# Attention, an MLP and a routed expert layer in one kernel: gating in a queue of its own, the last batch's scores in single halves, and row copies ahead of gating at unit ends

## The chip, the cores and the metric

The kernel runs on one core of one Trainium2 chip. The metric is device time in microseconds (us) for one execution. Before the change the median of three runs is 875.8 us (875.69 to 875.85). TensorE (PE in the profile) does matrix products, VectorE (DVE) and ScalarE (ACT) the elementwise work, GpSimd (POOL) small operations and indirect DMAs, SyncE (SP) issues most DMAs. Products are accumulated in PSUM, which has eight banks here: six that the program calls acc0 to acc4 and px, and two called ph.

## The reference

What is computed, cut to its core (batch 4, 8 heads, sequence 576, head size 64, 32 memory slots; 2304 tokens of 512; MLP width 2048; 8 experts of width 1024):

```python
a = softmax(phi, over the sequence)
k_m, v_m = einsum(a, k), einsum(a, v)             # 32 memory rows per head
x = softmax(q @ k_m.T / 8) @ v_m                  # attention onto the 32 rows
x = elu(x @ w_in) @ w_out                         # dense MLP, all 2304 rows
noisy = x @ w_gate + log1p(exp(x @ w_noise)) * noise
w = softmax(top2(noisy))                          # two experts for each token
out[t] = sum of w[t, e] * (relu(x[t] @ w1[e]) @ w2[e])
```

## The kernel before

The work is a list of iterations `flat`, numbered i. Iterations 0 to 63 belong to four MLP units, one for each batch (16 iterations each; the batches' rows lie in blocks of 4, 5, 4 and 5 tiles of 128 rows). Iterations 64 to 95 belong to four "early" expert units (256 rows of experts 0 to 3, 8 iterations each), 96 to 159 to the remaining rows of these experts and to experts 4 to 7. In iteration i TensorE does layer 1 of i (`layer1`, L976, in two halves of the columns for the MLP) and layer 2 of iteration i - 2 (`layer2`, L1026 to L1028, three products for each row tile; high and low parts of the operands stand for one full-precision product). VectorE closes layer 1 with the ELU (`elu_b`, L990 and L991, twice each) and writes low parts (L1009 of the hidden rows, L574 of the weights). A ph bank is free for layer 1 of i + 1 only when the ELU of i has read it.

Everything else is side work fitted into these iterations:

- `attention(b)` of the next batch: phi turned (L175), memory rows, then for b of 2 and 3 the transposed scores, in four quarters (h, g): `scores_t` (matmuls L314), its shift by the maximum (L322 to L324 on VectorE), an exponential on ScalarE, `normalize_t` (L335 to L338, on VectorE for b = 3), `turn_t` (L342) and `lower_t` (L347). `fold` (L488) multiplies v_m into four chunks of w_in every fourth iteration; `halve` then makes a high (L137, ScalarE) and a low part (L138, VectorE).
- `gating(blk)`: the block's x rows are read back (`reload`, L813), each tile is transposed (L650) and multiplied with the gate weights (`logits`, L640 and the copy L642); then come the top two experts (L683 to L790) and list entries (L799, one DMA for each tile and choice).
- `fetch` (list of a unit L863, row gathers L880) and `spread` (four TensorE transposes for each gathered tile, L895) prepare the first early unit and the first unit behind the early ones; `route` (gathers L920, L925, L931 and later transposes by VectorE) prepares the rest at fixed half-iterations held in `plan`.

These are Python generators in two queues, `heads` and `tails`. `tick(slot)` is called at three places of an iteration ("" ahead of layer 1's operations, "mid" behind its last matmul, "late" behind the ELU and the weights' low parts) and lets the first generator whose next step wants that slot take it, at most a step or two a slot. `later` holds a step's PSUM reads back to the end of the VectorE work of layer 1 (`settle`). POOL's paced DMAs (list entries, gathers of `fetch`) wait in `spaced`; `beat()` releases one of them by a tiny ScalarE operation (L616) and a POOL copy of it (L617). `drain(gen)`, called at the first iteration of a unit, first issues everything in `spaced`, then runs the generator that the unit needs to its end. In single-bank stretches (`single()`: batches with five acc tiles in use) side work has only px, and a fold's second half uses a ph bank. At the end of a unit its acc tiles are copied out (`put_rows`, L1034 and L1036 for the MLP, L1045 and L1047 for experts), behind what the last "late" slot issued.

## Time and profile before

| what | value |
|---|---|
| median of three runs | 875.8 us |
| profiled execution, its own time | 877.42 us |
| its span from first to last instruction | 875.7 us |
| TensorE busy | 843.8 us, 96% |
| VectorE busy | 567.3 us, 65% |
| ScalarE busy | 438.4 us, 50% |
| GpSimd busy | 202.6 us, 23% |
| granted TensorE clock, mean | 0.991 |

The durations below are those of one execution. Rows of a time view give the start in us from the beginning of the span, the duration in us, engine, source line, operation, output <- inputs by the program's names, tile shapes, and in brackets the idle time of that engine just before it with what ended it. A merged row (x2, x4) has one start and the time until its last one ended. Operations overlap in their pipelines, so the distance of two starts is the better price of one. A granted clock of 1.00 is TensorE's upper level of 2.4 GHz; a stretch with a mean below that ran partly at 1.2 GHz.

### The profile page before, as it was taken

How to read it: one execution, taken by the hardware profiler on the slowest of the kernel's cores; microseconds unless marked ns; L12 is line 12 of the kernel's file. 1: busy time of each engine (PE TensorE's matmuls, PEld its weight loads, DVE VectorE, ACT ScalarE, POOL GpSimd, SP SyncE). 2: the span in 40 equal slices, each digit the busy share in tenths (PEclk: the TensorE clock that was granted, in tenths of full speed). 3: DMA queues.
4: the chain of work that ended last, by engine and by line, in shares of the span. 5: the costliest groups of instructions: out<-in, count | busy, mean ns of one | idle time of the engine just before them, and what ended most of it. 6: DMA issues, size and time to landing. Idle time of an engine off the chain costs nothing. (4 is left out here: it accounts for less than half of the span.)

```text
span 875.7 us, 15408 instructions
## 1 busy us (share of the span) xinstructions
PE 843.8 (96%) x5688; PEld 698.4 (80%) x5691; DVE 567.3 (65%) x1200; ACT 438.4 (50%) x1007; POOL 202.6 (23%) x319
## 2 busy tenths in 40 slices
PE   8999999999998999979989999999999999999995
PEld 5566567777876778868778998888899999999994
DVE  5878887689768887766787765655657444454321
ACT  4767666555664555545646654544444333342311
POOL 1000100001323147124327421322412050120303
PEclk9999999999999999999999999999999999999998
DMA  9996678963852346453789987878996675452404
GB/s 349 345 385 224 220 272 285 329 222 141 295 172 86 97 148 142 110 180 121 206 229 216 286 247 240 235 236 244 287 247 186 181 166 170 142 122 97 59 1 60
DMA packets 100575, 174.65 MB, mean 199 GB/s; under 512 B 14610, under 2 KB 52370, under 8 KB 99474
## 3 DMA queue, kind: packets, MB, share of 16 engines
q1 hardware_dynamic: 90514, 152.93, 54.7%
q0 software_dynamic: 9984, 20.72, 12.0%
q8 instruction: 45, 0.74, 0.3%
q14 instruction: 32, 0.26, 0.1%
HBM read 132.01 MB, written 41.61 MB: 198 GB/s over the span
## 5 line engine op out<-in xcount | busy, mean ns | idle before, releaser
L1026 PE MATMUL acc<-bh,gl 128*128 128x512 f32 (+1 forms) x552 | 220.1, 399 | 1.5 <-DVE rows L1047 1.4
L1027 PE MATMUL acc<-bl,gh 128*128 128x512 f32 (+1 forms) x552 | 216.3, 392 | 0.0
L1028 PE MATMUL acc<-bh,gh 128*128 128x512 f32 (+1 forms) x552 | 216.0, 391 | 0.0
L1005 DVE SCALAR_TENSOR_TENSOR gl<-ph,gh 128x312 fp32r<-128x312 f32 (+2 forms) x128 | 61.6, 482 | 195.0 <-ACT gh L1004 194.9
L568 ACT ACTIVATE bh<-raw 128x512 fp32r<-128x512 f32 x144 | 90.0, 625 | 71.0 <-PE acc L1028 71.0
L1026 PEld LDWEIGHTS acc<-bh,gl 128*128 128x128 f32 (+1 forms) x552 | 103.0, 187 | 27.4 <-issue 7.5
L1028 PEld LDWEIGHTS acc<-bh,gh 128*128 128x128 f32 (+1 forms) x552 | 102.9, 186 | 23.6
L1004 ACT ACTIVATE gh<-ph 128x312 fp32r<-128x312 f32 (+2 forms) x128 | 55.0, 430 | 124.5 <-PE ph L976 124.5
L1027 PEld LDWEIGHTS acc<-bl,gh 128*128 128x128 f32 (+1 forms) x552 | 103.1, 187 | 17.3
L1049 POOL DMA_INDIRECT out<-rows,ids x40 | 65.0, 1624 | 203.6 <-DVE rows L1047 168.3
L574 DVE TENSOR_TENSOR bl<-raw,bh 128x512 fp32r<-128x512 f32 x144 | 99.0, 688 | 6.1 <-ACT bh L568 6.1
L976 PE MATMUL ph<-xl,ah 128*128 128x312 f32 (+2 forms) x512 | 94.4, 306 | 0.0
L976 PE MATMUL ph<-xh,al 128*128 128x312 f32 (+2 forms) x512 | 93.8, 305 | 0.0
L976 PE MATMUL ph<-xh,ah 128*128 128x312 f32 (+2 forms) x512 | 93.7, 305 | 0.0
L976 PEld LDWEIGHTS ph<-xl,ah 128*128 128x128 f32 x512 | 83.0, 188 | 8.2
L976 PEld LDWEIGHTS ph<-xh,al 128*128 128x128 f32 x512 | 79.1, 188 | 0.0
L976 PEld LDWEIGHTS ph<-xh,ah 128*128 128x128 f32 x512 | 78.8, 188 | 0.0
L976 PE MATMUL ph<-tl,fh 128*128 128x288 f32 x256 | 61.7, 323 | 5.9 <-DVE elu L991 3.2
L574 DVE TENSOR_TENSOR al<-raw,ah 128x512 fp32r<-128x512 f32 x96 | 65.5, 682 | 0.0
L920 POOL DMA_INDIRECT xg<-x2d,ids x35 | 37.2, 1064 | 120.8 <-DMA ids<-lst 70.1
L990 DVE SCALAR_TENSOR_TENSOR elu<-elu 128x288 f32<-128x288 f32 x128 | 58.4, 456 | 9.2 <-ACT elu L982 9.1
L981 ACT ACTIVATE elu<-ph 128x288 f32<-128x288 f32 x128 | 52.3, 408 | 22.4 <-PE ph L976 21.1
(265 smaller groups left out, 1230.4 us busy)
## 6 DMA issues: line engine op xcount, KB each, us to landing
raw<-in_wmoe SPq DMA_DIRECT2D x48, 1024.0 KB, 6.1
raw<-in_wmlp SPq DMA_DIRECT2D x32, 512.0 KB, 5.4
raw<-wxa SPq DMA_DIRECT2D x12, 1024.0 KB, 6.0
raw<-wxb SPq DMA_DIRECT2D x12, 1024.0 KB, 5.6
xs<-xg SPq DMA_DIRECT2D x35, 256.0 KB, 6.4
xq<-xs SPq DMA_DIRECT2D x140, 64.0 KB, 4.9
kv<-in_kv SPq DMA_DIRECT2D x8, 1024.0 KB, 13.1
out<-zrow SPq DMA_DIRECT2D x13, 512.0 KB, 9.4
```

The costliest lines, as they stand in the source:

```text
L568: act.activation(ready[h, c][0], raws[h, c], AF.Copy)
L574: dve.tensor_tensor(lo, raws.pop((h, c)), hi.bitcast(F32), op=OP.subtract)
L920: pool.indirect_dma_start(out=xg, out_offset=None, in_=x2d[:rows], in_offset=bass.IndirectOffsetOnAxis(ap=n["ids"][:, t, 0:1], axis=0))
L976: pe.matmul(ph, w, x, start=k == 0, stop=k == len(terms) - 1)
L981: act.activation(t[:, 0, o], ph, AF.Exp)
L990: dve.scalar_tensor_tensor(m, t[:, 0, o], 1.0, m, op0=OP.add, op1=OP.mult)
L1004: act.activation(gh[:, o], ph, AF.Relu)
L1005: dve.scalar_tensor_tensor(gl[:, o], ph, 0.0, gh[:, o].bitcast(F32), op0=OP.max, op1=OP.subtract)
L1026: pe.matmul(acc, gl[:, o], wh, start=f == 0, stop=False)
L1027: pe.matmul(acc, gh[:, o], wl, start=False, stop=False)
L1028: pe.matmul(acc, gh[:, o], wh, start=False, stop=f == u["nf"] - 1)
L1049: d = pool.indirect_dma_start(out=out, out_offset=bass.IndirectOffsetOnAxis(ap=ids[:m, t, 0:1], axis=0), in_=r, in_offset=None, compute_op ...
```

## The change

Six edits; line numbers of the changed kernel differ from those above.

1. The per-tile part of gating (transpose, logits) becomes a generator `tiles` in a third queue `sides`; `gating` waits until its block's tiles are done. `sides` gets slots after the other two queues and can start while attention steps hold `heads`.
2. For b = 3 the scores are issued one quarter (h, g) an iteration instead of two, and their shift is put into `behind`, which is emptied behind the ELU.
3. `fetch` of the first early unit ends two steps later (`after` = 2), so that its `spread` starts later.
4. Where a unit ends, the "late" slot and its beat come behind `put_rows`.
5. `drain` issues beats only while the wanted generator is still queued.
6. A fold's halves change banks (the first half uses ph in single-bank stretches), and a fold inside layer 2 at a unit's first iterations comes after four tiles rather than three.

```diff
-    deferred, place = [], [""]
+    deferred, behind, place = [], [], [""]
...
             for g in gs:
-                later(lambda g=g: shift(g))
+                if place[0] == "mid" and not single():
+                    behind.append(lambda g=g: shift(g))
+                else:
+                    later(lambda g=g: shift(g))
...
-                    scores_t(h)
-                    yield "light"
-                    grow_t(h, 0)
-                    grow_t(h, 1)
-                    if h == 0:
-                        yield "mid"
+                    for g in range(2):
+                        scores_t(h, [g])
+                        yield "late"
+                        grow_t(h, g)
+                        if (h, g) != (1, 1):
+                            yield "mid"
...
-        bks = {g: bank("ph", 2) if single() and g else side_bank() for g in gs}
+        bks = {g: side_bank() if g or not single() else bank("ph", 2) for g in gs}
...
-    heads, tails, moe = [], [], {}
+    heads, tails, sides, moe = [], [], [], {}
...
-        for queue in (heads or tails, tails):
+        went = False
+        for queue in (heads or tails, tails, sides):
+            if queue is sides and slot == "mid" and not taken and not (went and single()):
+                kinds = {"mid"}
...
-                want = wants.get(id(gen)) or ("next" if gen.__name__ == "fetch" else "pe")
+                want = wants.get(id(gen)) or {"fetch": "next", "tiles": "late"}.get(gen.__name__, "pe")
...
     def drain(gen):
         place[0] = ""
-        while spaced:
-            beat()
         for queue in (heads, tails):
             while gen in queue:
+                while spaced:
+                    beat()
...
+    def tiles(blk, rows):
+        lg = att["lg", blk] = sm.tile([P, 5, 2 * NE], F32, tag="lg", name="lg", bufs=2)
+        for tt in range(BLOCKS[blk][1]):
             while tt >= len(rows):
                 yield "late"
             yield "late"
             x2T = rp.tile([P, 4, P], F32, tag="x2T", name="x2T", bufs=1)
             dve.transpose(x2T.rearrange("p g (a s) -> p a g s", s=32), rows[tt].rearrange("p a (g d) -> p a g d", d=32))
             yield "mid"
-            logits(tt, x2T, 1)
+            bk = side_bank()
+            logits(bk, x2T, 1)
+            later(lambda bk=bk, tt=tt: dve.tensor_copy(lg[:, tt, :], bk[:, :16]))
+        att["tiles", blk] = True
+
+    def gating(blk, rows):
...
+        while blk < 3 and ("tiles", blk) not in att:
+            yield "next"
...
-            if t == 3 and between:
+            if t == 3 + (f == 0) and between:
...
-                        (tails if k == 3 else heads).extend([fetch(n, [n]), n["need"]] if k == 3 else [n["need"]])
+                        (tails if k == 3 else heads).extend([fetch(n, [n], 2), n["need"]] if k == 3 else [n["need"]])
...
                 settle()
+                for f_ in behind:
+                    f_()
+                behind.clear()
...
-            tick("late")
-            if u["kind"] == "mlp":
-                beat()
+            ends = i >= LAG and pend[0][1] == pend[0][0]["nf"] - 1
+            if not ends:
+                tick("late")
+                if u["kind"] == "mlp":
+                    beat()
...
+                        sides.append(tiles(b, back))
...
+                if i < len(flat):
+                    tick("late")
```

What VectorE has in its row between the low parts of iteration 38 and the ELU of iteration 40, before (L322 to L324 are a quarter's shift, L990 and L991 the ELU, L1009 and L574 the low parts):

```order
L574 TENSOR_TENSOR bl<-raw,bh 128x512
L322 STREAM_TRANSPOSE sbt<-px 128x288
L323 TENSOR_REDUCE smx<-sbt 128x9
L324 TENSOR_TENSOR sbt<-sbt,smx 128x288
L322 STREAM_TRANSPOSE sbt<-acc_3138 128x288
L323 TENSOR_REDUCE smx<-sbt 128x9
L324 TENSOR_TENSOR sbt<-sbt,smx 128x288
L990 SCALAR_TENSOR_TENSOR elu<-elu 128x288
L991 SCALAR_TENSOR_TENSOR elu<-ph,elu 128x288
L990 SCALAR_TENSOR_TENSOR elu<-elu 128x288
L991 SCALAR_TENSOR_TENSOR elu<-ph,elu 128x288
L1009 TENSOR_TENSOR gl<-elu,gh 128x512
```

The same place in the changed kernel (L1006 and L1007 are the ELU, L652 a gating tile's transpose, L785 a gating reciprocal, L656 a logits copy):

```order
L1006 SCALAR_TENSOR_TENSOR elu<-elu 128x288
L1007 SCALAR_TENSOR_TENSOR elu<-ph,elu 128x288
L1006 SCALAR_TENSOR_TENSOR elu<-elu 128x288
L1007 SCALAR_TENSOR_TENSOR elu<-ph,elu 128x288
L322 STREAM_TRANSPOSE sbt<-px 128x288
L323 TENSOR_REDUCE smx<-sbt 128x9
L324 TENSOR_TENSOR sbt<-sbt,smx 128x288
L785 RECIPROCAL g_rec<-g_den 128x4
L652 STREAM_TRANSPOSE x2T<-xr 128x4x4x32
L1025 TENSOR_TENSOR gl<-elu,gh 128x512
L577 TENSOR_TENSOR bl<-raw,bh 128x512
L656 COPY lg<-acc_3262 128x16
```

Two shifts stood ahead of an ELU; now one stands behind it, with gating's transpose and copy in the same iteration.

ScalarE at the start of iteration 64, the first of the early units, before (L568 makes high parts of weights, L1004 the ReLU, L1034 copies rows out):

```order
L997 ACTIVATE gh<-elu 128x576
L1000 ACTIVATE gh<-rest 128x64
L616 ACTIVATE beat<-top 1x1 x8
L568 ACTIVATE ah<-raw 128x512
L568 ACTIVATE bh<-raw 128x512
L1004 ACTIVATE gh<-ph 128x256
L568 ACTIVATE ah<-raw 128x512
L568 ACTIVATE bh<-raw 128x512
L1004 ACTIVATE gh<-ph 128x256
L1034 ACTIVATE rows<-acc_4009 128x512
```

And in the changed kernel (L571, L1020, L1050 and L623 stand for L568, L1004, L1034 and L616):

```order
L1013 ACTIVATE gh<-elu 128x576
L1016 ACTIVATE gh<-rest 128x64
L571 ACTIVATE ah<-raw 128x512
L571 ACTIVATE bh<-raw 128x512
L1020 ACTIVATE gh<-ph 128x256
L571 ACTIVATE ah<-raw 128x512
L571 ACTIVATE bh<-raw 128x512
L1020 ACTIVATE gh<-ph 128x256
L623 ACTIVATE beat<-top 1x1
L1050 ACTIVATE rows<-acc_4017 128x512
```

The eight beats in a row are gone from there; single beats stand in the iterations behind.

GpSimd around the first early unit's two gathers (L880), before (L617 is a beat's copy, L799 a list entry, L690 a gating copy, L920 a routed unit's gather):

```order
L617 COPY tiny<-beat 1x1
L799 DMA lst<-g_rec,g_slot 19328x2
L690 COPY g_rec<-tokid 128x4 x2
L920 DMA xg<-x2d,ids 128x512
L617 COPY tiny<-beat 1x1
L880 DMA xg<-x2d,ids 128x512
L617 COPY tiny<-beat 1x1
L880 DMA xg<-x2d,ids 128x512
L920 DMA xg<-x2d,ids 128x512 x2
```

And in the changed kernel (L624, L815, L706, L896 and L936 in the place of these):

```order
L624 COPY tiny<-beat 1x1
L815 DMA lst<-g_rec,g_slot 19328x2
L624 COPY tiny<-beat 1x1
L896 DMA xg<-x2d,ids 128x512
L706 COPY g_rec<-tokid 128x4 x2
L624 COPY tiny<-beat 1x1
L896 DMA xg<-x2d,ids 128x512
L936 DMA xg<-x2d,ids 128x512 x4
```

Both gathers now stand ahead of the routed unit's and are released in iteration 58 rather than 59. The transposes that read them (`spread`) stood at the end of iteration 59 and inside 60 in TensorE's row; they now stand at the end of 60 and inside 61.

## Rows read from the trace of the kernel before

**Rows 1.** TensorE waits: who <- what it waited for: us, times, longest
```profile
PE px L895 <- DMA xg<-x2d,ids: 4.5, 1, 4.5
PE ph L976 <- DVE elu L991: 3.2, 3, 1.8
PE px L661 <- DVE rows L1036: 1.9, 1, 1.9
PE ph L976 <- DVE fl L138: 1.7, 3, 0.8
PE acc L1026 <- DVE rows L1047: 1.4, 1, 1.4
PE acc L640 <- DVE x2T L650: 1.0, 1, 1.0
```

**Rows 2.** stretches: length, busy us (count) by engine, clock, DMA, GB/s
```profile
234.00:314.00 80.00, 75.41 (x677) 58.50 (x677) 65.11 (x156) 44.38 (x129) 22.73 (x58) 0.98 0.44 130
375.00:393.00 18.00, 13.54 (x70) 11.89 (x69) 10.42 (x30) 6.64 (x18) 4.75 (x6) 0.91 0.70 220
```

**Rows 3.** TensorE in time: start us, us, line, operation, count; fold of iteration 50
```profile
326.63 1.04 PE L488 MATMUL px<-raw,vT 64*32 64x512 f32 x2
```

**Rows 4.** TensorE in time: scores by halves (batch 2), then by pairs (batch 3)
```profile
173.48 0.69 PE L314 MATMUL px<-q,kmF 64*32 64x288 f32 x8
174.10 0.50 PE L1026 MATMUL acc<-bh,gl 128*128 128x512 f32 x1
...
268.87 0.43 PE L314 MATMUL px<-q,kmF 64*32 64x288 f32 x1
...
269.52 0.50 PE L1026 MATMUL acc<-bh,gl 128*128 128x512 f32 x1
```

**Rows 5.** TensorE in time: first matmuls of iterations 36, 48 and 49
```profile
242.24 0.51 PE L976 MATMUL ph<-tl,fh 128*128 128x288 f32 x2
...
313.82 0.46 PE L976 MATMUL ph<-tl,fh 128*128 128x288 f32 x2
...
318.18 0.42 PE L976 MATMUL ph<-tl,fh 128*128 128x288 f32 x2
```

**Rows 6.** VectorE in time: start us, us; iterations 39 and 42
```profile
264.64 0.48 DVE L322 STREAM_TRANSPOSE sbt<-acc 128x288 f32<-128x288 f32 x1
...
266.02 0.45 DVE L990 SCALAR_TENSOR_TENSOR elu<-elu 128x288 f32<-128x288 f32 x1
...
284.40 0.45 DVE L990 SCALAR_TENSOR_TENSOR elu<-elu 128x288 f32<-128x288 f32 x1
...
286.11 0.45 DVE L335 TENSOR_REDUCE ssu<-sbt 128x9 f32<-128x288 f32 x1
...
287.43 0.70 DVE L650 STREAM_TRANSPOSE x2T<-xr 128x512 f32<-128x512 f32 x1
288.06 0.65 DVE L138 TENSOR_TENSOR fl<-px,fh 128x512 fp32r<-128x512 f32 x1
...
289.23 0.81 DVE L347 TENSOR_TENSOR tl<-back,th 128x288 fp32r<-128x288 f32 x2
...
289.95 0.68 DVE L1009 TENSOR_TENSOR gl<-elu,gh 128x512 fp32r<-128x512 f32 x1
...
291.24 0.45 DVE L990 SCALAR_TENSOR_TENSOR elu<-elu 128x288 f32<-128x288 f32 x1
```

**Rows 7.** GpSimd in time: the second gather of the first early unit
```profile
381.38 0.97 POOL L880 DMA_INDIRECT xg<-x2d,ids  x1 [0.48 <-issue]
```

**Rows 8.** ScalarE in time: beats at the start of iteration 64
```profile
408.43 0.46 ACT L616 ACTIVATE beat<-top 1x1 f32<-1x1 f32 x4
...
414.12 0.20 ACT L616 ACTIVATE beat<-top 1x1 f32<-1x1 f32 x1 [1.11 <-POOL tiny L617]
```

**Rows 9.** VectorE in time: a row copy of the first early unit
```profile
450.67 0.74 DVE L1047 TENSOR_SCALAR rows<-acc,ids 128x512 f32<-128x512 f32 x1
```

**Rows 10.** GpSimd in time: a routed unit's gather
```profile
518.95 0.99 POOL L920 DMA_INDIRECT xg<-x2d,ids  x1 [17.04 <-DMA xs<-xg]
```

More of the change, by code (lines that the diff above doesn't have):

```diff
@@ L601, in tick @@
                 stepped[id(gen)] = i
+                went = True
                 try:
@@ L629, in drain, with logits @@
                     wants.pop(id(queue.pop(0)), None)
-    def gating(blk, rows):
-        t0, nt = BLOCKS[blk]
-        lg = sm.tile([P, 5, 2 * NE], F32, tag="lg", name="lg")
-        def logits(tt, x2T, turned):
-            bk = side_bank()
-            for c in range(4):
-                for j in range(0, P, 32):
-                    pe.matmul(bk[j:j + 32, :16], x2T[:, c, j:j + 32], wgs[:, turned, c, :], start=c == 0, stop=c == 3,
-                              tile_position=(0, j))
-            later(lambda: dve.tensor_copy(lg[:, tt, :], bk[:, :16]))
-        x2T = None
-        for tt in range(nt if blk < 3 else 0):
+    def logits(bk, x2T, turned):
+        for c in range(4):
+            for j in range(0, P, 32):
+                pe.matmul(bk[j:j + 32, :16], x2T[:, c, j:j + 32], wgs[:, turned, c, :], start=c == 0, stop=c == 3,
+                          tile_position=(0, j))
+    def tiles(blk, rows):
+        lg = att["lg", blk] = sm.tile([P, 5, 2 * NE], F32, tag="lg", name="lg", bufs=2)
+        for tt in range(BLOCKS[blk][1]):
             while tt >= len(rows):
@@ L651, in gating @@
             yield "mid"
-            logits(tt, x2T, 1)
+            bk = side_bank()
[3 more added lines that the diff above has]
+    def gating(blk, rows):
+        t0, nt = BLOCKS[blk]
+        x2T = None
+        while blk < 3 and ("tiles", blk) not in att:
+            yield "next"
+        if blk == 3:
+            att["lg", blk] = sm.tile([P, 5, 2 * NE], F32, tag="lg", name="lg", bufs=2)
+        lg = att["lg", blk]
         for tt in range(nt + 1 if blk == 3 else 0):
             if tt:
-                logits(tt - 1, x2T, 0)
+                bk = side_bank()
+                logits(bk, x2T, 0)
+                later(lambda bk=bk, tt=tt: dve.tensor_copy(lg[:, tt - 1, :], bk[:, :16]))
                 if len(banks["tags"]) == 1:
```

## The prediction

> **What bounds the kernel now.** The table of engines comes first: TensorE is busy for 96% of the span, VectorE for 65%. So the time is TensorE's work, its few idle gaps, and what it loses at a low clock. The second view is TensorE's waits [rows 1]. The gaps that the change can touch are 4.5 us of `spread` for a gather, 3.2 us of layer 1 for the ELU (three times, the longest 1.8), 1.9 us of the last block's turn for a row copy, 1.7 us of layer 1 for the folded weights' low part (three times), 1.4 us of layer 2 for an expert's row copy, and 1.0 us of the logits for a transposed tile. The third view is the table of stretches [rows 2]: the mean clock is 0.98 over 234 to 314 and 0.91 over 375 to 393. At 1.2 GHz work takes twice as long as at 2.4, so a missing share of 0.02 in 80 us is 1.6 us lost, and 0.09 in 18 us is also 1.6. In each of the two lies one of the longest gaps (1.8 and 4.5 us); with a gap gone I count its clock loss as gone too. Then I read TensorE and VectorE in time inside those stretches.
>
> Waits and clock together are 13.7 + 3.2 = 16.9 us; that is the pool from which the change can draw, apart from TensorE work that it adds.
>
> **The change part by part.**
>
> *Folds (edit 6).* In single-bank stretches the folded half that layer 1 wants first was the second to be lowered; now it is the first. Two low parts take 1.17 us (288.06 to 289.23 in [rows 6]), so one of them 0.6. Of the three waits of 1.7 us in all [rows 1] two are longer than that: each falls by 0.6, the third (0.1 to 0.2) goes. In iteration 50 the fold also stands one tile later; its first matmuls take 1.04 us there [rows 3], while their partners wait for the ELU to free a ph bank. How much of it is waiting no other row here shows: bounds 0 and 1.0; I take 0.7. Sum: 0.6 + 0.6 + 0.15 + 0.7 = -2.0.
>
> *Scores and gating tiles (edits 1 and 2).* Iterations 36 to 47 take 313.82 - 242.24 = 71.6 us [rows 5], a bare one 318.18 - 313.82 = 4.4. In 39 and 40 two shifts of 1.38 us each (264.64 to 266.02) stand ahead of the ELU, and the next layer 1 waits for it. After the change only one shift an iteration is left, behind the ELU. VectorE then has in 39: ELU 1.7, shift 1.4, transpose 0.6, low parts 1.2 and small things, about 5.2; TensorE has 4.4 + 0.6 (scores) + 0.5 (logits) = 5.5 there. So the waits there go: -3.2 of the ELU waits, -1.0 at the logits, whose transpose is done an iteration ahead, and the clock loss of 1.6. Removed: 5.8.
>
> What is added is, first, TensorE work. A quarter issued alone takes 174.10 - 173.48 = 0.62 us, a pair 269.52 - 268.87 = 0.65 [rows 4]. Two pairs become four single quarters: 4 x 0.62 - 2 x 0.65 = +1.2. The Trainium skill ("TensorE: Matmul & The Clock Gate", section "Why this matters for your kernels", small-K matmuls) says that products with a short contraction which lie in separate row groups run at the same time, which speaks against splitting them. The trace agrees, 0.65 for a pair beside 0.62 for one; without that rule the split would cost nothing, and the sum would be 1.2 lower.
>
> Second, VectorE's work is not less, it is later. From [rows 6]: ELU 284.40 to 286.11 = 1.7; a normalization to 287.43 = 1.3; a transposed gating tile 0.6; two folded low parts 1.2; two lowers (289.23 to 289.95) 0.7, and two turns, which have the same shape, 0.7 too; the iteration's low parts and a logits copy to 291.24 = 1.3. By the order, iteration 42 has ELU, shift, folded parts, normalization, low parts: 1.7 + 1.4 + 1.2 + 1.3 + 1.2 = 6.8. 43 has ELU, normalization, turns, low parts: 4.9 and a small reciprocal; 44 the lowers instead of the turns, 4.9; 45 normalization and turns, 4.9; 46 lowers, two gating steps, folded parts, low parts, 5.6. In all 27.1 or a little more. TensorE has in 42 to 46 five bare iterations, 22.0, two folds of 1.1 and one quarter, 24.8. VectorE becomes the bound there, by at least 27.1 - 24.8 = 2.3 us. It also stands idle in 42 until the fold, which ends the iteration, has been read by ScalarE: no row gives the price of that at this place, so 0 and 2.2 bound it. New waits: 2.3 to 4.5; I take 3.0, since iteration 41 leaves VectorE a lead of under one us. Sum of the stretch: -5.8 + 1.2 + 3.0 = -1.6, with -4.6 (none) and -0.1 as ends. The reloads that feed gating's transposes are issued as before; the transposes come up to three iterations earlier. If one came before its data, the wait would be of the size of the 1.0 at the logits [rows 1]; I count nothing.
>
> *First early unit (edit 3).* The second gather is issued at 381.38 [rows 7] and its transposes wait 4.5 us. After the change the gathers are released an iteration earlier and read one later, two iterations or some 10 us more between them, so the wait goes whole, and with it the clock loss of 375 to 393: -4.5 - 1.6 = -6.1. Nothing else waits on them: the unit's first layer 1 is three iterations behind the last transpose.
>
> *Beats at 64 (edit 5).* Eight beats hold ScalarE from 408.43 to 414.32 [rows 8], each waiting for GpSimd's copy. ScalarE's ReLUs come late, VectorE's row copies behind them too, and the turn waits 1.9 us [rows 1]. With the flush gone ScalarE goes on at 408.5. Bounds: 0, if VectorE is late for another reason, and 1.9 and the end of the lateness. I take -1.9.
>
> *Row copies first (edit 4).* The copy at 450.67 takes 0.74 us [rows 9] behind six small gating operations, and layer 2 waits 1.4 for it. The copy itself stays, so the wait falls to 0.7 at best: -0.7. At the other unit ends no such wait is in [rows 1]; there late work, gating's POOL and ScalarE steps among it, only goes behind.
>
> Sum: -2.0 - 1.6 - 6.1 - 1.9 - 0.7 = -12.3. The profiled execution, 877.42 by its own time (span 875.7), would come to 865.1; the median of the runs lies 1.6 below the profiled execution, 875.8 - 12.3 = 863.5.
>
> **The rivals.**
>
> *R1, no new wait on VectorE.* If the shifts and normalizations of 42 to 47 fit (the engine starts 42 with a lead, and each ELU is needed only at the next layer 1's end of ph), the 3.0 goes: 860.5. For it: VectorE's share of the stretch is 65.1 of 80 us [rows 2]. Against: the sum of 27.1 beside 24.8.
>
> *R2, the clock falls again.* New waits in 43 to 47 that gather into one of 1.8 us or more cost 1.6 each, as the old ones did [rows 1, 2]: 865.1, and with two 866.7. The skill ("TensorE: Matmul & The Clock Gate", section "HAM oscillation — how this bites in real kernels") tells of kernels that pay such a fall again in every loop, behind waits for data. Here the traces show two falls; without that sentence the rival stands on [rows 2].
>
> *R3, edit 3 doesn't do what it says.* If the gathers, released by beats, wait for their list and slide along with the transposes, the 6.1 stays: 869.6. Against: GpSimd's order has both ahead of a routed gather that stood between them.
>
> *R4, slower: beats against GpSimd's waits.* The eight list entries flushed at 64 are now spread over 66 to 70, in the row of GpSimd with routed gathers. Such a gather has held GpSimd 17.0 us, until its data was stored [rows 10]. If one stands between two beats, the ring of four beats fills, ScalarE stops at the next beat, and its ReLUs with it; TensorE runs on to the end of its iteration on its two ph banks, half a bare iteration or 2.2 us in the mean [rows 5]. 17.0 - 2.2 = 14.8 us: 863.5 + 14.8 = 878.3. From a hold of 14.5 us on the kernel is slower than before (12.3 + 2.2). Against: that hold is at 519, where a unit of five tiles is routed; near 420 there is none among TensorE's waits.
>
> **How the numbers follow.** The forecast 0.54, R1 0.16, R2 0.13, R3 0.08, R4 0.07, others 0.02 (of it half slower). Forecast 863.5, by its own bounds 860 to 867 (the fold's 0.7, the beats' 1.9, VectorE's 2.3 to 4.5). R1 and R2 lie inside or near 859 to 867; R3 takes the upper end to 870; R1 with the higher gains of the folds and beats takes the lower one to 858. The range is 858 to 870. A measurement of this kernel tells 0.2%, 1.75 us, from no change. Faster by more than that: everything below 874, 0.54 + 0.16 + 0.13 + 0.08 less an allowance of 0.04 for two mishaps together, 0.87. Slower, above 877.6: half of R4 and others with what ends there, 0.08; the rest, 0.05, lies within.
>
> **What would show it.** In the profile after: no wait at `spread`, a clock of 1.00 over the last MLP iterations (edit 3); no eight beats at the start of 64 and no wait at the last block's first turn (edit 5); layer 1's waits for the folded low part at 0.3 or less (edit 6); one wait of about 0.7 where layer 2 follows the first early unit's row copies; in 36 to 47 some 70 us, with no layer 1 waiting for the ELU in 39 to 41 and small waits for it in 43 to 47. A mean clock above 0.995 says that no fall came back. What would prove me wrong: a wait for the ELU that is as long as before in 39 to 41, a wait at `spread`, or a TensorE gap behind 66 that ends with ScalarE.

## The result and the profile after

The changed kernel takes 866.5 us (median of four runs, 866.2 to 867.1) beside 875.75 for the kernel before: a ratio of 0.990, with a 95% interval of 0.988 to 0.992, or 9.2 us. Forecast were 863.5, inside a range of 858 to 870, and 12.3. The profiled execution of the changed kernel took 866.58 us with a span of 864.8; its mean clock is 0.998.

The engines' line of the page after:

```profile
PE 840.4 (97%) x5688; PEld 695.7 (80%) x5691; DVE 567.5 (66%) x1200; ACT 438.3 (51%) x1007; POOL 205.5 (24%) x319
```

TensorE's waits after, the view of [rows 1] (who <- what it waited for: us, times, longest). The program's lines are shifted by up to 16: L992 is layer 1, L1007 the ELU, L768 and L770 the count products of gating, L1042 layer 2, L1063 an expert's row copy.

```profile
PE ph L992 <- DVE elu L1007: 4.7, 4, 1.7
...
PE acc L768 <- DVE fl L138: 1.5, 1, 1.5
PE acc L770 <- DVE g_oh L759: 1.2, 1, 1.2
...
PE acc L1042 <- DVE rows L1063: 0.5, 1, 0.5
PE ph L992 <- DVE fl L138: 0.5, 1, 0.5
```

The 4.5 us at `spread` and the 1.9 at the last block's turn are gone, the folded low part is down from 1.7 to 0.5, the row copy from 1.4 to 0.5. But the waits for the ELU, 3.2 before, are 4.7, and 1.5 us are new, at gating's count products (L768; the 1.2 at L770 stood in the kernel before too, at its L754). The stretches that answer to [rows 2], same columns:

```profile
234.00:310.00 76.00, 71.58 (x666) 55.83 (x650) 62.20 (x153) 44.48 (x128) 26.14 (x59) 1.00 0.44 130
365.00:390.00 25.00, 25.00 (x151) 21.10 (x150) 20.07 (x58) 14.69 (x40) 6.74 (x10) 1.00 0.54 179
```

The clock is 1.00, the upper level, in both, where it was 0.98 and 0.91. TensorE in time (start, duration, in brackets the wait before), the start of iteration 36 and the waits of 36 to 47:

```profile
239.66 0.51 PE L992 MATMUL ph<-tl,fh 128*128 128x288 f32 x2
...
259.99 0.18 PE L768 MATMUL acc<-run,ones 128*128 128x40 bf16 x1 [1.47 <-DVE fl L138]
...
288.87 0.50 PE L992 MATMUL ph<-tl,fh 128*128 128x288 f32 x2 [1.25 <-DVE elu L1007]
...
294.62 0.53 PE L992 MATMUL ph<-tl,fh 128*128 128x288 f32 x2 [1.17 <-DVE elu L1007]
...
299.80 0.54 PE L992 MATMUL ph<-tl,fh 128*128 128x288 f32 x2 [0.53 <-DVE elu L1007]
...
311.74 0.50 PE L992 MATMUL ph<-tl,fh 128*128 128x288 f32 x2 [1.72 <-DVE elu L1007]
```

The first is the start of iteration 36, the last the start of 48: 311.74 - 239.66 = 72.1 us, beside 71.6 in [rows 5].

To see where the time went, I cut the runs' traces at TensorE's first layer 1 product of an iteration; in us:

| iterations | before | changed | difference | forecast |
|---|---|---|---|---|
| up to 15 | 124.7 | 123.7 | -1.0 | 0 |
| 16 to 35 | 117.5 | 116.0 | -1.5 | -1.2 |
| 36 to 47 | 71.6 | 72.1 | +0.5 | -1.6 |
| 48 to 55 | 44.2 | 42.7 | -1.4 | -0.8 |
| 56 to 62 | 44.7 | 38.4 | -6.4 | -6.1 |
| 63 to 74 | 50.2 | 48.0 | -2.2 | -2.6 |
| 75 to 95 | 60.65 | 61.2 | +0.6 | 0 |
| 96 to 127 | 129.2 | 128.9 | -0.3 | 0 |
| 128 to 158 | 209.1 | 210.5 | +1.4 | 0 |

The first line is scatter: up to 15 the programs have the same work, and over all profiles here that part ran from 122.5 to 125.8. Without it the sum is -9.3; the end of the program, behind the start of 159, is another 0.5 shorter. Against the forecast two things are missing: 2.1 us in 36 to 47, and 1.7 in the expert iterations, where I had expected nothing to change.

### The profile page after: what moved, and what is told of

Same layout as the page of the kernel before. It is cut to its first block, busy times and chain, and to the rows that moved or that the text cites. A ratio compares the mean times of both kernels' runs of the same rounds, so it can differ in the third digit from the quotient of the medians.

```text
span 864.8 us, 15414 instructions
## 1 busy us (share of the span) xinstructions
PE 840.4 (97%) x5688; PEld 695.7 (80%) x5691; DVE 567.5 (66%) x1200; ACT 438.3 (51%) x1007; POOL 205.5 (24%) x319
## 5 line engine op out<-in xcount | busy, mean ns | idle before, releaser
L1042 PE MATMUL acc<-bh,gl 128*128 128x512 f32 (+1 forms) x552 | 219.6, 398 | 0.6 <-DVE rows L1063 0.5
L571 ACT ACTIVATE bh<-raw 128x512 fp32r<-128x512 f32 x144 | 89.9, 624 | 72.5 <-PE acc L1044 72.4
L1042 PEld LDWEIGHTS acc<-bh,gl 128*128 128x128 f32 (+1 forms) x552 | 102.8, 186 | 26.2 <-issue 6.5
L1020 ACT ACTIVATE gh<-ph 128x312 fp32r<-128x312 f32 (+2 forms) x128 | 54.8, 428 | 126.1 <-PE ph L992 125.9
L992 PE MATMUL ph<-xl,ah 128*128 128x312 f32 (+2 forms) x512 | 95.2, 308 | 0.0
L992 PE MATMUL ph<-xh,al 128*128 128x312 f32 (+2 forms) x512 | 94.2, 306 | 0.0
L992 PE MATMUL ph<-xh,ah 128*128 128x312 f32 (+2 forms) x512 | 93.5, 305 | 0.0
L992 PEld LDWEIGHTS ph<-xl,ah 128*128 128x128 f32 x512 | 83.5, 189 | 8.9
L992 PEld LDWEIGHTS ph<-xh,al 128*128 128x128 f32 x512 | 79.4, 188 | 0.0
L992 PEld LDWEIGHTS ph<-xh,ah 128*128 128x128 f32 x512 | 78.9, 188 | 0.0
L992 PE MATMUL ph<-tl,fh 128*128 128x288 f32 x256 | 60.5, 317 | 6.3 <-DVE elu L1007 4.7
L1006 DVE SCALAR_TENSOR_TENSOR elu<-elu 128x288 f32<-128x288 f32 x128 | 58.5, 457 | 9.4 <-ACT elu L998 9.4
L936 POOL DMA_INDIRECT xg<-x2d,ids x35 | 37.3, 1066 | 112.7 <-DMA ids<-lst 70.4
L1013 ACT ACTIVATE gh<-elu 128x576 fp32r<-128x576 f32 (+1 forms) x50 | 33.0, 660 | 58.4 <-DVE elu L1007 58.4
```

Of the source, the lines that this page charges most:

```text
L571: act.activation(ready[h, c][0], raws[h, c], AF.Copy)
L936: pool.indirect_dma_start(out=xg, out_offset=None, in_=x2d[:rows], in_offset=bass.IndirectOffsetOnAxis(ap=n["ids"][:, t, 0:1], axis=0))
L992: pe.matmul(ph, w, x, start=k == 0, stop=k == len(terms) - 1)
L1006: dve.scalar_tensor_tensor(m, t[:, 0, o], 1.0, m, op0=OP.add, op1=OP.mult)
L1013: act.activation(gh[:, o], m, AF.Copy)
L1020: act.activation(gh[:, o], ph, AF.Relu)
```

## The experiments

All times are medians, beside the kernel before in the same group of runs. There are three groups: in the first (the four kernels down to the count products) the kernel before took 878.5 us, in the others 875.8 and 875.4, so times are compared within a group, or as ratios. Runs with profile have their stretches in the table behind the experiments.

**One edit alone, on the kernel before.** Edit 3:

```diff
-extend([fetch(n, [n]), n["need"]]
+extend([fetch(n, [n], 2), n["need"]]
```

> The kernel before with edit 3 alone: the first early unit's transposes stand one to two iterations later, its gathers where they were. Theory (the parts of the change add up): the 4.5 us wait and the clock fall behind it go, -6.1 us beside the kernel before, and iterations 59 to 62 have no wait. Rival (the wait goes only because the gathers also came earlier, by edit 1): a wait of 1 us or more is left, -3 to -5 us.

874.7 us beside 878.5, ratio 0.995 (0.993 to 0.996). The 3.8 us lie in the rival's range, but the wait that the rival leaves isn't there: nothing waits at `spread`, and 56 to 62 take 39.4 instead of 44.7, -5.4. So edit 3 does it without the earlier gathers. But 63 to 74 take 52.9 rather than 50.2. TensorE in time there:

```profile
415.64 0.66 PE L661 MATMUL px<-ident,rows 128*128 128x128 f32 x4 [2.52 <-DVE bl L574]
...
417.22 1.06 PE L976 MATMUL ph<-xh,ah 128*128 128x256 f32 x4
```

The turn of the last block waits 2.5 instead of 1.9, and four products of 256 columns behind it last 1.06 in all where four before them last 0.71: a fall to 1.2 GHz that the kernel before had not here. Whether the edit brings these 2.7 us is not shown: the kernels of this group are long there whatever the edit (below), and the kernel before has no profile in this group.

Edit 6:

```diff
-bks = {g: bank("ph", 2) if single() and g else side_bank() for g in gs}
+bks = {g: side_bank() if g or not single() else bank("ph", 2) for g in gs}
...
-if t == 3 and between
+if t == 3 + (f == 0) and between
```

> The kernel before with edit 6 alone: the first needed half of a fold uses the ph bank, and the fold of iteration 50 stands one tile later. Theory: the three waits for the folded low part fall by 1.3 us and the fold of 50 gains up to 1.2, -2.0 to -2.7 us. Rival (the fold's gain in the changed kernel came from VectorE's lighter load by edits 1 and 2): less than 1 us.

877.3 us beside 878.5, ratio 0.998 (0.997 to 1.000). 16 to 35 give 1.5, all of what the change gives there, 48 to 55 give 0.6 of the 1.4; the rest of it comes with edits 1 and 2, which take six small gating operations of VectorE out of 48 to 51. By the stretches, 2.1 together, the theory holds at its lower end; the time alone, 1.3 shorter with an interval of 0.4 to 2.5, does not tell it from the rival. The trace has one thing more, in a stretch that this edit does not touch:

```profile
142.37 0.53 PE L976 MATMUL ph<-tl,fh 128*128 128x288 f32 x2 [0.51 <-DVE fl L138]
...
419.15 0.66 PE L661 MATMUL px<-ident,rows 128*128 128x128 f32 x4 [1.49 <-issue]
```

The first row is the wait for the folded low part, 0.83 before. The second is a wait of 1.5 for nothing that the profile shows. Edits 3 and 6 alone take 2.7 and 3.5 us more in 63 to 74 than the kernel before elsewhere, the count step later (below) 3.4 more than the changed kernel elsewhere, and three of the four kernels of this group have waits of this kind (0.85 to 1.5). I come back to it in the last section.

Edits 1 and 2 (the other four undone in the changed kernel):

```diff
-extend([fetch(n, [n], 2), n["need"]]
+extend([fetch(n, [n]), n["need"]]
...
-        bks = {g: side_bank() if g or not single() else bank("ph", 2) for g in gs}
+        bks = {g: bank("ph", 2) if single() and g else side_bank() for g in gs}
...
-            if t == 3 + (f == 0) and between:
+            if t == 3 and between:
...
-            ends = i >= LAG and pend[0][1] == pend[0][0]["nf"] - 1
+            ends = False
...
-                if i < len(flat):
-                    tick("late")
```

and `drain` as before.

> The kernel before with edits 1 and 2 alone (gating tiles in their own queue, the last batch's scores by quarters). Theory: the waits for the ELU only move from iterations 39 to 41 to 43 to 47, and a new wait of 1.5 us stands at gating's count step behind the fold of iteration 38, so no gain: between -0.5 and +1 us. Rival (the prediction's sum, with the missing microseconds lost elsewhere): -1.6 us or more.

875.4 us beside 878.5, ratio 0.996 (0.995 to 0.997). The 3.1 us are the rival's number, but not for its reason: 36 to 47 take 72.5, +0.9, as the theory had it; what falls is 56 to 62, by 3.9, and iteration 65, from 7.3 to 5.25. TensorE at the first early unit's transposes, and GpSimd's two gathers for them:

```profile
370.52 0.63 PE L911 MATMUL px<-ident,xg 128*128 128x128 f32 x4 [1.32 <-DMA xg<-x2d,ids]
```

```profile
366.82 1.12 POOL L896 DMA_INDIRECT xg<-x2d,ids  x1 [1.22 <-issue]
...
369.32 0.98 POOL L896 DMA_INDIRECT xg<-x2d,ids  x1 [0.50 <-issue]
```

With gating's tiles in their own queue the entries of the list are done earlier, the gathers go out some twelve us earlier (the second at 369.3 rather than 381.4 [rows 7]), and the wait is 1.3 instead of 4.5, though the transposes come earlier too, in 57 and 58. It is edit 1 that does this: with edit 2 undone (below) the gathers are issued in 57 and 58 too, with edit 3 alone in 59 and 60. So edits 1 and 3 both act on this wait: -3.9 with edits 1 and 2, -5.4 with edit 3 alone, together -6.4. And the eight beats at 64 are gone with edits 1 and 2, though `drain` is as before.

**The count products.** The changed kernel with one step moved:

```diff
-        yield "next" if blk < 2 else "pe"
+        yield "next" if blk == 1 else "pe"
```

> The changed kernel with one step moved: the count products of the first block's gating want the slot that a fold closes, so they stand an iteration behind the fold of 38 and not right behind it. Theory: the 1.5 us wait for the folded low part at the count step goes and nothing takes its place: 865.0 us, 1.5 below the changed kernel. Rival (the wait is slack that layer 1 of 39 would have spent anyway, waiting for the same VectorE row): same time, and a wait of 1 us or more at layer 1 of iteration 39 or 40.

867.9 us beside 878.5, ratio 0.988 (0.986 to 0.989); the changed kernel's is 0.990 (0.988 to 0.992) in its own groups, so the times alone do not show a gain. Inside the stretch the theory holds: iteration 38 goes from 7.7 to 6.0, 39 from 5.6 to 5.8, 36 to 47 from 72.1 to 70.5. The two banks that side work has there, acc4 and px, both hold the fold; the count products are next in TensorE's row and need one of them, so they wait until ScalarE and VectorE have read it. What is left, and this group's wait for nothing:

```profile
286.95 0.50 PE L992 MATMUL ph<-tl,fh 128*128 128x288 f32 x2 [1.07 <-DVE elu L1007]
...
413.87 0.45 PE L642 MATMUL acc<-wgs,x2T 128*32 128x16 f32 x32 [0.85 <-issue]
```

**The changed kernel again, and its addresses.**

> The changed kernel itself, once more, so that the next kernels have it beside them on the same chip. Theory and rival alike: 0.987 to 0.992 of the kernel before.

866.6 us beside 875.8; ratio 0.990 (0.988 to 0.991).

```diff
+    sm.tile([P, 48], F32, tag="pad", name="pad")
```

> The changed kernel with an unused tile of 192 bytes a partition among the small tiles, so that the tiles behind them lie 512 bytes from where they lay in the kernel before, rather than 320. Nothing else differs. Theory: the second logits buffer of the change moved the expert operands, and their matmuls became slower by that (an iteration of 256 rows 2.82 to 2.85 us instead of 2.79, one of 624 rows 6.88 instead of 6.83, some 27 and 31 of them); with the pad they are back at 2.79 and 6.83, the kernel 2 to 2.4 us faster than the changed one. Rival (the expert iterations are slower for another reason, such as DMA traffic moved by the change): same iterations, same time.

864.7 us beside 866.6, ratio to before 0.987 (0.985 to 0.989). First products of early iterations and of two late ones, TensorE in time; before, after, and with the pad:

```profile
435.65 0.63 PE L976 MATMUL ph<-xl,ah 128*128 128x256 f32 x4
...
438.44 0.63 PE L976 MATMUL ph<-xl,ah 128*128 128x256 f32 x4
...
653.76 0.73 PE L976 MATMUL ph<-xl,ah 128*128 128x312 f32 x4
...
660.59 0.74 PE L976 MATMUL ph<-xl,ah 128*128 128x312 f32 x4
```

```profile
424.29 0.65 PE L992 MATMUL ph<-xl,ah 128*128 128x256 f32 x4
...
427.13 0.64 PE L992 MATMUL ph<-xl,ah 128*128 128x256 f32 x4
...
429.95 0.65 PE L992 MATMUL ph<-xl,ah 128*128 128x256 f32 x4
...
642.04 0.75 PE L992 MATMUL ph<-xl,ah 128*128 128x312 f32 x4
...
648.92 0.75 PE L992 MATMUL ph<-xl,ah 128*128 128x312 f32 x4
```

```profile
424.73 0.63 PE L994 MATMUL ph<-xl,ah 128*128 128x256 f32 x4
...
427.52 0.63 PE L994 MATMUL ph<-xl,ah 128*128 128x256 f32 x4
...
430.31 0.63 PE L994 MATMUL ph<-xl,ah 128*128 128x256 f32 x4
...
642.19 0.74 PE L994 MATMUL ph<-xl,ah 128*128 128x312 f32 x4
...
649.02 0.74 PE L994 MATMUL ph<-xl,ah 128*128 128x312 f32 x4
```

Distances of starts: 256 rows, 2.79 before, 2.84 and 2.82 after, 2.79 and 2.79 with the pad; 624 rows, 6.83, 6.88 and 6.83. 75 to 95 and 128 to 158 are back at 60.7 and 209.1. The theory holds: the second buffer of `lg` moved everything behind the small tiles by 320 bytes, and these iterations pay 0.7 to 1.8% for it. Not all expert operands lie behind the small tiles: by the addresses in the built programs the rows and the weights of layer 1 moved, the hidden rows and the weights of layer 2 did not. 192 bytes that nobody uses give 1.9 us by the medians, 1.7 by the stretches. The next run says more: its unused tile of 768 bytes makes the shift 1088, and 75 to 95 and 128 to 158 take 61.2 and 210.6 there, as in the changed kernel.

**VectorE as the bound of 43 to 47.** Three fills (`junk`, 192 columns) of 0.26 us, 0.78 together, behind the ELU of five iterations of the changed kernel:

```diff
                 behind.clear()
+                if i in (39, 40, 41, 44, 45):
+                    for _ in range(3):
+                        dve.memset(junk, 0.0)
```

> The changed kernel with three small extra VectorE fills (a few tenths of a us together) behind the ELU of iterations 39, 40, 41, 44 and 45. The computation is the reference's. Theory (VectorE bounds 43 to 47 and not 39 to 41): iterations 39 to 41 stay at 5.5 to 5.6 us, 44 and 45 grow by what the fills take. Rival (the waits in 43 to 47 come from ScalarE's or GpSimd's side of the chain): all five stay as they are.

868.75 us in one run, +2.2; 36 to 47 take 74.5, +2.5. The fills on VectorE in 41 and 44, then TensorE's waits at the starts of 44, 46 and 47:

```profile
277.37 0.87 DVE L1230 MEMSET junk<- 128x192 f32 x3
...
295.45 0.87 DVE L1230 MEMSET junk<- 128x192 f32 x3
```

```profile
288.92 0.50 PE L993 MATMUL ph<-tl,fh 128*128 128x288 f32 x2 [1.68 <-DVE elu L1008]
...
300.80 0.53 PE L993 MATMUL ph<-tl,fh 128*128 128x288 f32 x2 [1.46 <-DVE elu L1008]
...
307.11 0.54 PE L993 MATMUL ph<-tl,fh 128*128 128x288 f32 x2 [0.64 <-DVE elu L1008]
```

39 and 40 stay at 5.62 and 5.52; 41 grows by 0.2, and 43 by 0.4, with the wait at the start of 44 from 1.25 to 1.68. 45 and 46 grow by 0.95 and 0.7, together 1.65 for 1.6 of fills in 44 and 45: as the theory had it, one iteration later than it said. So VectorE is the bound from 43 on and has slack ahead of it. The slack is small: the fills of 39 and 40 cost nothing, and of the 0.78 in 41 about 0.65 comes out.

**Edit 2 undone in the changed kernel** (scores in pairs again, shifts ahead of the ELU):

```diff
-                if place[0] == "mid" and not single():
-                    behind.append(lambda g=g: shift(g))
-                else:
-                    later(lambda g=g: shift(g))
+                later(lambda g=g: shift(g))
...
-                    for g in range(2):
-                        scores_t(h, [g])
-                        yield "late"
+                    scores_t(h)
+                    yield "light"
```

> The changed kernel with edit 2 undone (the last batch's scores in pairs, their shifts ahead of the ELU), edit 1 kept. Theory (edit 2 only moves VectorE's excess from 39 to 41 into 43 to 47): waits of 1.2 us or more for the ELU at the starts of 40 and 41 with a clock below 1.00 behind them, none above 0.6 in 44 to 48, iterations 36 to 47 within 1.5 us of the changed kernel's 72.1, the time within 1.5 us of it. Rival (edit 2 is what removes the clock fall and costs nothing that stood before): 3 us or more slower than the changed kernel.

867.2 us beside 875.4, ratio 0.990 (0.989 to 0.991), as the changed kernel's. 36 to 47 take 72.4. The times are the theory's; the waits are not where it had them:

```profile
271.21 0.45 PE L639 MATMUL acc<-wgs,x2T 128*32 128x16 f32 x32 [1.50 <-DVE sbt L322]
...
291.98 0.65 PE L989 MATMUL ph<-tl,fh 128*128 128x288 f32 x2 [2.30 <-DVE elu L1004]
...
292.90 0.68 PE L989 MATMUL ph<-th,fh 128*128 128x288 f32 x2
```

```profile
234.00:310.00 76.00, 70.12 (x658) 55.59 (x658) 62.93 (x157) 43.74 (x127) 25.16 (x60) 0.98 0.42 120
```

TensorE waits 0.6 and 1.5 at the logits in 39 and 40, for the shift that still reads their bank, not for the ELU; and 2.3 in one piece at the start of 44, after which the clock falls to 1.2 GHz (a pair of products of 288 columns 0.68 rather than 0.43; mean clock 0.98 over the stretch, 1.00 with edit 2). So edit 2 turns waits of 0.6, 1.5 and 2.3 into four of at most 1.7, of about the same sum. It saves a clock fall and pays for it with TensorE work; the stretch is as long.

**Edit 5 undone in the changed kernel:**

```diff
         place[0] = ""
+        while spaced:
+            beat()
         for queue in (heads, tails):
             while gen in queue:
-                while spaced:
-                    beat()
```

> The changed kernel with edit 5 undone (all spaced DMAs issued at the start of 64). Theory: the few beats left there hold ScalarE again and iteration 65 goes from 5.24 back to about 7.3: +2 us. Rival (fewer beats are spaced at 64 since gating is later, so the flush is short): under 0.7 us.

867.4 us, ratio 0.991 (0.989 to 0.992). The rival holds, and further than it went: the built program has the same instructions in the same order on every engine as the changed kernel. At 64 nothing is spaced any more: with edits 1 and 2 the eight list entries come into the queue later, and go out one or two at a time in 65 to 70. It is therefore a third measurement of the changed kernel, and says that a median here is good to about 1 us.

**Combined versions.** The pad, the count step, the second block's gating delayed by two iterations, and the fold's lowering put behind the side step that follows:

```diff
-                place[0] = ""
+                place[0] = "mid"
                 fold(j // 4, j % 4, [0, 1])
             tick("", turn_ if i > 13 else i % 2 == 0)
+            settle()
...
-        for _ in range(3 if eng is pool else 0):
+        for _ in range(5 if eng is pool and blk else 3 if eng is pool else 0):
```

> The changed kernel with four edits: the pad; the first block's count step one slot later; the second block's gating steps two iterations later, out of 46; and a fold's lowering put behind the side step that follows it, so that a normalization fills VectorE's wait for the fold in 42. Theory: -2.2 (pad), -1.5 (count step), -1.2 (wait of 1.25 at iteration 44), -1.5 (wait of 1.72 at iteration 48): 860 us on the chip where the changed kernel takes 866.5, a ratio of 0.983 to the kernel before. Rival (the waits for the ELU only move on to the next iterations, since the steps of the chain are the same in number): pad and count step alone, ratio 0.986.

863.25 us, ratio 0.986 (0.984 to 0.988): the rival's number, but not for its reason. 36 to 47 fall to 68.7, -3.4 (iteration 43 from 5.8 to 4.4, 47 from 6.3 to 5.5, 38 from 7.7 to 6.0). Given back are 0.4 in 35, 0.35 in 36, 0.9 in 50 and 51, and 1.75 in 62 and 63, where one of the first early unit's gathered tiles is now transposed and count products wait (0.6 of it has only moved there, out of 60 and 61):

```profile
392.63 0.18 PE L772 MATMUL px<-g_oh,tri 128*128 128x32 bf16 x1 [0.94 <-DVE g_oh L761]
```

The next version confines the fold's delay to one fold and shortens `fetch` by one step; the one behind it keeps the delay of that fold, the pad and the count step alone:

```diff
-                place[0] = ""
+                place[0] = "mid" if i == 43 else ""
...
-fetch(n, [n], 2)
+fetch(n, [n], 1)
```

> The combined kernel with two of its edits cut to where they pay: the fold's lowering behind the side step at iteration 42 alone, and the first early unit's fetch one step shorter, so that its transposes stand at the ends of 60 and 61 as in the changed kernel. Theory: keeps the combined kernel's gains in 38, 43 and 47 (1.7, 1.4, 0.8) and the pad's 1.9, and loses none of the 0.75 in 35 and 36, 0.9 in 50 and 51, 1.4 in 60 to 63: 861 us where the changed kernel takes 866.5, ratio 0.983. Rival: its second gather is issued about 5 us ahead of its transposes, and lands later, a wait of 1 to 2 us at 61: 862 to 863.

> As the one before, without the two iterations' delay of the second block's gating steps, and with the fetch as in the changed kernel. Theory: the wait of about 1.7 at the start of 48 stays, no risk at 61: 861.8 us, ratio 0.984. Rival: as the waits of 43 to 47 hang together, the wait at 48 grows by what 44 gains (1.4): 863.

The two take 862.8 and 863.1 us beside 875.4, ratios 0.985 (0.984 to 0.986) and 0.985 (0.984 to 0.987). Both are faster than either kernel of the case; between themselves they cannot be told apart. The times are the two rivals' numbers, for other reasons. The first has 68.3 in 36 to 47 and 38.4 in 56 to 62 without a wait at `spread`, so its rival's cause falls; the second has 69.2 in 36 to 47. Its theory holds: the wait at the start of 48 is 1.74, no more than in the changed kernel. The waits for the ELU left in the first:

```profile
292.48 0.53 PE L994 MATMUL ph<-tl,fh 128*128 128x288 f32 x2 [1.11 <-DVE elu L1009]
...
297.67 0.53 PE L994 MATMUL ph<-tl,fh 128*128 128x288 f32 x2 [0.51 <-DVE elu L1009]
...
308.81 0.50 PE L994 MATMUL ph<-tl,fh 128*128 128x288 f32 x2 [0.95 <-DVE elu L1009]
```

The forecasts of 861 and 861.8 were too low by 1.8 and 1.3. In the first of the two, two stretches are not as forecast: 50 and 51 are still 0.9 longer than in the changed kernel, and 96 to 127 are 0.4 longer than with the pad alone, for a cause that stays open. The second has neither, and its wait at the start of 48 is 1.74 instead of 0.95. So delaying the second block's gating only moves VectorE's work for it: 0.8 won at 48 and 0.9 lost at 50 and 51. The stretches of the second are as forecast. The rest is the start: the profiled spans, 861.9 and 861.4, began with 124.4 and 124.7 us up to 15, and the changed kernel's with 123.5 and 123.7. That part scatters, as said.

| us in iterations | 16 to 35 | 36 to 47 | 48 to 55 | 56 to 62 | 63 to 74 | 75 to 95 | 96 to 127 | 128 to 158 |
|---|---|---|---|---|---|---|---|---|
| before | 117.5 | 71.6 | 44.2 | 44.7 | 50.2 | 60.65 | 129.2 | 209.1 |
| changed | 116.0 | 72.1 | 42.7 | 38.4 | 48.0 | 61.2 | 128.9 | 210.5 |
| edit 3 alone | 117.5 | 71.6 | 44.2 | 39.4 | 52.9 | 60.7 | 129.2 | 209.1 |
| edit 6 alone | 116.1 | 71.6 | 43.6 | 45.8 | 53.8 | 60.65 | 129.2 | 209.1 |
| edits 1 and 2 alone | 117.5 | 72.5 | 43.45 | 40.9 | 51.25 | 61.8 | 129.0 | 210.55 |
| changed, count step later | 116.1 | 70.5 | 42.7 | 38.4 | 51.4 | 61.3 | 129.0 | 210.6 |
| changed, pad | 116.1 | 72.0 | 42.75 | 38.4 | 47.9 | 60.7 | 129.2 | 209.1 |
| changed, edit 2 undone | 116.05 | 72.4 | 43.0 | 38.4 | 47.7 | 61.2 | 129.0 | 210.6 |
| combined, second version | 116.0 | 68.3 | 43.6 | 38.4 | 48.0 | 60.6 | 129.65 | 209.1 |

## Why the prediction came out as it did

The forecast came out, 3.0 us low: by the stretches it missed 2.1 in 36 to 47 and 1.7 in the expert iterations, and the other parts gave 0.8 more than forecast.

**The first early unit (edit 3), forecast -6.1, measured -6.4 in 56 to 62.** Wait and clock fall went as the working had it. Alone the edit gives 5.4 there; that edits 1 and 2 give 3.9 by themselves was in the text only as "the gathers are released an iteration earlier".

**Scores and gating tiles, forecast -1.6, measured +0.5.** This is the step that failed, in two of its terms. "Removed: 5.8" holds, and is even 6.3: no layer 1 waits for the ELU in 39 to 41 and the clock is 1.00; gone are 4.6 us of waits, 0.4 at a second logits product among them, and 1.7 at the low clock. The added term, "new waits: 2.3 to 4.5; I take 3.0", is 1.25 + 1.17 + 0.53 + 1.72 = 4.7. VectorE after the fold of 42, in the changed kernel, shows why:

```profile
284.02 0.69 DVE L138 TENSOR_TENSOR fl<-acc,fh 128x512 fp32r<-128x512 f32 x1 [1.60 <-ACT fh L137]
...
285.22 0.45 DVE L338 TENSOR_REDUCE ssu<-sbt 128x9 f32<-128x288 f32 x1
...
286.54 0.69 DVE L1025 TENSOR_TENSOR gl<-elu,gh 128x512 fp32r<-128x512 f32 x1
...
287.77 0.46 DVE L1006 SCALAR_TENSOR_TENSOR elu<-elu 128x288 f32<-128x288 f32 x1
...
289.50 0.44 DVE L338 TENSOR_REDUCE ssu<-sbt 128x9 f32<-128x288 f32 x1
...
291.12 0.78 DVE L345 STREAM_TRANSPOSE back<-sbt 128x288 f32<-128x288 f32 x2
...
293.54 0.53 DVE L1006 SCALAR_TENSOR_TENSOR elu<-elu 128x288 f32<-128x288 f32 x1
```

The folded low part can begin only 1.6 us after VectorE is free, at 284.02; with the two low parts, the normalization and the low parts of the iteration the ELU of 43 starts at 287.77, and that of 44 at 293.54, 5.8 later, where a bare iteration of TensorE is 4.4. The idle piece that I bounded by 0 and 2.2 and mostly left out is there, and no later iteration has room to make it good. Between the ELU of 46 and that of 47 stand six small gating operations, 1.2 us, where the working had two steps for some 0.8; VectorE has as many fewer in 48 to 51, so a part of the wait at the start of 48 has its counterpart in the -1.4 of 48 to 55. The place was right and the size was not. The other term I did not have at all: the count products behind the fold, 1.5 us. The working counted what the change queues up on VectorE and not what it puts behind what on TensorE's side banks. The trace after shows the fold and the count products in consecutive rows, on the same bank. The split into quarters was too dear in the working: instead of +1.2 it comes to some +0.6, an estimate from what is left of the balance, 0.5 + 6.3 - 4.7 - 1.5. The price of a pair was read from the second one, 0.65; the first took 1.00 (261.85 to 262.85 in TensorE's row before).

Under both terms lies one assumption: that what TensorE saves in this stretch shortens it. The kernel before shows otherwise. Edit 3 alone leaves 36 to 47 as they were; the same waits of 1.25 and 1.80 stand there at the starts of 40 and 41, but this time no fall of the clock follows. The stretch by engine, first in the kernel before, then with edit 3 alone (columns as in [rows 2]):

```profile
242.24:313.82 71.58, 66.99 (x621) 52.11 (x620) 57.82 (x140) 39.34 (x115) 22.55 (x58) 0.98 0.39 119
```

```profile
243.04:314.60 71.56, 65.64 (x621) 51.00 (x620) 57.82 (x140) 39.22 (x115) 22.57 (x58) 1.00 0.40 118
```

At the upper level TensorE works 1.35 us less and waits 1.33 more, in 42 and 43 for a transpose and a low part of VectorE, and the stretch is as long; edit 6 alone shows the same, 71.6 at a clock of 1.00. So the 1.6 us that the working counted for the clock here were worth nothing by themselves. TensorE's work does not set the length of this stretch; its waits end with VectorE, which has eight small gating operations more there in the changed kernel, 59.6 us of work instead of 57.8.

**Folds, forecast -2.0, measured -1.5 in 16 to 35 and -1.4 in 48 to 55.** Right in place; the 48 to 55 part is only half the edit's own, by the run of edit 6 alone, which makes the edit's sum 2.1. The sign that the working named, waits for the folded low part of 0.3 or less, did not come: the longest fell from 0.83 to 0.49.

**Beats at 64, forecast -1.9, measured -2.1 in iteration 65.** Right in time and wrong in cause, so the number is luck as far as edit 5 goes: undoing it changes no instruction here, and edits 1 and 2 take the eight beats away without it. Reading the built order of ScalarE told me that the eight beats were gone, not which edit had taken them away.

**Row copies first, forecast -0.7, measured -0.85 in iteration 74.** The wait is 0.5 where 0.7 was said. I did not run this edit alone; but the wait is still 1.4 with edit 3 alone, with edit 6 alone and with edits 1 and 2 alone, and edit 5 changes nothing, which leaves edit 4.

**The expert iterations, forecast 0, measured +1.7.** No step of the prediction looked at addresses. The run with the pad shows them to be the whole of it, the -0.3 in 96 to 127 included: with the pad 75 to 95, 96 to 127 and 128 to 158 are back at 60.7, 129.2 and 209.1.

Of the rivals R1 (no new wait on VectorE) fell with the 4.7 us. R2 did not come: four waits of 0.5 to 1.7 in 43 to 47, and the clock stayed at its upper level. With edit 2 undone the same stretch has one wait of 2.3 and behind it a fall, in which a pair of products of 288 columns takes 0.68 us for 0.43; the time is the same as without it. The Trainium skill ("TensorE: Matmul & The Clock Gate", section "HAM oscillation — how this bites in real kernels") says that a kernel in which TensorE stands idle long enough pays again in products at half the clock; the trace agrees, with a granted clock of 1.2 GHz behind the 2.3. R3 fell, R4 too: ScalarE waits nowhere for a beat behind 66.

## What to carry to other kernels

A wait that a slower engine causes is not gone when its work is put elsewhere in the same chain: add up that engine's work between two deadlines, with its own idle pieces in it, and compare with what the fast engine has there. Where the slower engine sets the pace, a clock fall of the fast one may cost nothing, as in 36 to 47 here, so count it as a gain only where no wait stands ready to take its place. Look in the new order for steps that now stand directly behind one another on the same PSUM bank. When a change adds or widens a buffer, look at iterations that it does not touch: if they are all slower by the same small part, it may be the addresses, and a run with a pad tells.

## What the runs showed of the hardware

- With the operands of layer 1 of the experts (weights and rows) 320 bytes further, TensorE's iteration of 256 rows takes 2.82 to 2.85 us instead of 2.79 and that of 624 rows 6.88 instead of 6.83; 1088 bytes further it is the same, and 512 bytes further it is 2.79 and 6.83 again. Iterations of 368 rows hardly change (4.07 and 4.08). Whether it is the weights or the rows stays open; they moved together, while layer 2's operands stayed where they were.
- In the first group of runs 63 to 74 were 2.7 to 3.5 us longer than in the others for the three kernels that can be compared. Three of its four kernels have TensorE waits of 0.85 to 1.5 us there that the profile puts down to nothing, and three have a fall of the clock there (to 1.2 GHz). The changed kernel with the count step later has the same instructions there as the changed kernel, which took 48.0 rather than 51.4. The record names another chip for each group; no run separates that from other causes. The cause stays open; it is why times of that group are not set beside those of others.
- Waits of 1.25, 1.17, 0.53 and 1.72 us within 25 us left the clock at its upper level; one of 2.30 in the same stretch was followed by products at 1.2 GHz for about 3 us. The waits of 1.25 and 1.80 at the starts of 40 and 41 were followed by such a fall in the kernel before and by none with edit 3 alone: the length of a wait alone does not tell whether the clock falls.
